# Queries copied by GpSimd one unit sooner in an attention backward loop, their transposing DMA ahead of the second score transpose of a block

## The chip, the cores and the metric

One core of one Trainium2 chip. The metric is the device time of the slowest (here the only) core, in microseconds. The engines: PE does matmuls (PEld loads their weights), DVE, ACT and POOL (GpSimd) work elementwise, SP issues DMAs. Each engine takes its instructions in order, and waits on semaphores for the others.

## What is computed

Two attention blocks on a sequence of 2048 tokens of 448 features with 16 heads of 28, and the gradients of all their inputs. Block A is linear attention, block B softmax attention with one key head and one value head for all query heads. The change lies in block B's loop:

```python
q = (x @ wq).reshape(B, S, H, Dh)        # 16 heads
k = x @ wk                               # one head of keys
v = x @ wv                               # one head of values
scores = einsum("bhqd,bkd->bhqk", q, k) * Dh ** -0.5
p = softmax(scores)
o = einsum("bhqk,bkd->bhqd", p, v)
b = o.reshape(B, S, H * Dh) @ wo
# the output is concatenate([a, b]); vjp(grad_out) gives the gradients of x, wq, wk, wv, wo of both blocks
```

With E the exponentials of the scores and dS = E * (v . do - D), the loop makes o (E with v), dv (E with do), dq (dS with k) and dk (dS with q) for each pair of heads.

## The kernel before, in words

The first fifth of the time is block A and what block B's loop needs; it is not touched. Then a loop written out by hand, with its order fixed (`manual_schedule`, line 922), runs over *units* u = 0 to 539 (line 931). A unit is 256 keys (two tiles of 128) of one *block*; a block is 256 queries of one pair of heads and has 8 units, so there are 64 blocks and 512 units of scores. Later stages of the same unit of work come later in the loop: the gradient of unit w = u - 16, the transpose of unit y = u - 18, and so on. In a unit:

- PE makes the scores of u and the products v . do of w (`rows_SD`, line 683), and by parity of u the sums for o and dq (`o_dq`, line 894) or those of dk (`dk_m`, line 865).
- ACT takes the exponentials of the two score banks into eT (lines 955 and 997), and copies one bank of v . do into cp (line 971).
- DVE multiplies the other bank by eT into half 0 of dsT (line 967); POOL multiplies cp by eT into half 1 (line 972). dsT has 5 buffers, cp has 3.
- DVE transposes dsT of unit u - 18 in 32 x 32 blocks into dsx (line 1041), that is, two units after POOL's product of the same piece. dsx feeds dk on PE.
- After units 3 and 7 of a block SP issues a transposing DMA, eN from eT of four units (line 999; 1 MiB). eN feeds dv on PE: `dv_mm` (line 901) for block b begins at unit 8b + 20. There are 5 buffers of eT and 6 of eN.
- Once a block, on POOL: prod (line 821), don and o (lines 830 and 831) in unit 2 of the following stage, Dq and its product (lines 836 and 837) in unit 4. In every fourth block or so POOL also issues an output DMA (line 749).
- After blocks 15, 31, 47, 55 and 63 SP issues a transposing DMA of the outputs o (line 1048).

dk needs the queries in another layout, qX, made anew for each chunk of 256 queries (eight blocks, 64 units); there are two buffers of it. For each of four groups g of heads, POOL copies the queries in two halves into a staging tile qst (`qc_copy`, lines 854 to 857; called at line 979), and one transposing DMA on SP's queue brings qst into qX (`qc_T`, lines 859 to 861; called at line 1002). There is **one buffer** of qst (line 709), so the first copy of a group waits until the DMA of the group before has read it. The first chunk is made ahead of the loop (lines 924 to 930); the other seven in blocks 3 to 6 of each eight, four groups each, 28 in all, up to unit 447 (`u < 448`). The first dk that reads a new qX comes 27 units after its chunk's first unit.

The places of copies and DMA follow from one line: in unit u, `gq` is the group and `iq` the unit counted from the group's first; copies run at iq 0 and 1, behind the product of the same unit on POOL, and the DMA is issued at iq 1, behind the eN transpose if the unit has one.

```python
gq, iq = divmod(u % 64 - 30, 8)
...
    if iq < 2:
        qc_copy(nc.gpsimd, qst, qq, gq, iq)
...
    if u % 4 == 3:
        nc.sync.dma_start_transpose(ENs[u // 4 % 6][:, :, :],
...
    if 0 <= gq < 4 and iq == 1 and u < 448:
        qc_T(qst, qq, gq)
```

Before, the copies stand in units 6 and 7 of a block, and the DMA in unit 7 behind that unit's eN transpose.

Of the kernel before, what the change touches and what calls it, by code (L numbers as in the profile page):

```python
# [25 lines left out]
def kernel(  # L26
# [624 lines left out]
    with ExitStack() as cs_:  # L651
# [270 lines left out]
        with tc.manual_schedule():  # L922
# [8 lines left out]
            for u in range(NU + 28):  # L931
# [31 lines left out]
                if hasD:  # L963
# [6 lines left out]
                    cp = pc_.tile([P, 512], BF16, name="cp")  # L970
                    nc.scalar.activation(out=cp[:, :], in_=dp[1][:, :], func=ACT.Copy)  # L971
                    nc.gpsimd.tensor_tensor(out=dst[:, 1, :], in0=cp[:, :], in1=ew[:, 1, :], op=ALU.mult)  # L972
                gq, iq = divmod(u % 64 - 30, 8)
                qq = u // 64 + 1
                if 0 <= gq < 4 and u < 448:
                    if gq == 0 and iq == 0:
# [183 lines left out]
```

## Time and profile before

| | |
|---|---|
| median of 3 runs | 1047.6 us (1046.28 to 1047.8) |
| the profiled execution | 1045.81 us, its span 1044.1 us |
| granted TensorE clock | 1.0 |
| busy: PE, DVE, ACT, POOL | 1003.6, 887.4, 865.8, 811.9 us |
| POOL's products, line 972 | 512 at 1156 ns mean |
| POOL's copies into qst, line 856 | 56 at 613 ns mean |
| eN transposes issued by SP, line 999 | 128, median 5422 ns each |
| qst transposes issued by SP, line 860 | 28, median 1264 ns each |
| DMA traffic | 195.15 MB, mean 187 GB/s |

How to read it: the profile lists busy time by engine and by line of the kernel, and for each group of instructions the idle time of its engine ahead of them, with what ended it. A row of SP's queue (SPq) is the time that SP takes to issue the transfer; when it has landed is told by the completion events of its semaphore. An arrow out<-in names the tile written and those read. "[2.11 <-X]" behind a row of the timeline is idle time of that engine before it, and X ended it as far as the profile can tell.

### The profile page before, as it was taken

The page shows a single profiled execution, that of the slowest core. Times are in us where ns is not written, and L with a number is a line of the kernel's source. Part 1 is how long each engine was busy: PE and PEld are TensorE (multiplying, and loading weights), DVE is VectorE, ACT ScalarE, POOL GpSimd, SP SyncE. Part 2 cuts the span into 40 slices and gives each one's busy share as a digit, 9 for nine tenths or more (in the row PEclk, how much of TensorE's full clock was granted, in tenths as well). Part 3 has the DMA queues.
Part 4 walks back from the last instruction along what each step waited for, and adds up shares of the span by engine and source line. Part 5 has one row for each costly group of instructions (what it writes and reads, how often), then busy time and mean ns, then how long its engine had stood idle before and what let it go on. Part 6 is the DMA issues. An engine that isn't in the chain of part 4 may idle for free.

```text
span 1044.1 us, 40103 instructions
## 1 busy us (share of the span) xinstructions
PE 1003.6 (96%) x16236; PEld 485.1 (46%) x16245; DVE 887.4 (85%) x1780; ACT 865.8 (83%) x1743; POOL 811.9 (78%) x1106
## 2 busy tenths in 40 slices
PE   9999999998899999999999999999999999999998
PEld 5555555434444444444444444444444444444444
DVE  7898500669899999999999999999999999999942
ACT  6463132599999999999999999999999999999632
POOL 8601282238898999999999989999998999888860
PEclk9999999999999999999999999999999999999999
DMA  9879999199999999999999999999999999999983
GB/s 266 150 134 195 184 232 213 32 161 205 189 183 198 191 188 195 198 190 189 201 198 197 190 190 203 194 193 198 202 184 201 191 199 192 192 194 197 218 159 90
DMA packets 689059, 195.15 MB, mean 187 GB/s; under 512 B 670409, under 2 KB 686689, under 8 KB 688873
## 3 DMA queue, kind: packets, MB, share of 16 engines
q1 hardware_dynamic: 680392, 179.97, 103.7%
q0 software_dynamic: 4544, 9.46, 3.1%
q10 hardware_dynamic: 3936, 3.16, 1.1%
q8 instruction: 127, 2.08, 0.8%
q14 instruction: 60, 0.48, 0.2%
HBM read 12.60 MB, written 10.84 MB: 22 GB/s over the span
## 4 chain that ended last, share of the span: by engine, by line
PE 37%; DVE 28%; POOL 17%; issue 9%; ACT 8%; DMA 0%; DVEq 0%; POOLq 0%; ACTq 0%
PE agen L81 13%; POOL dsT L972 12%; DVE dsT L967 12%; DVE dsx L1041 10%; PE agen L676 8%; PE aacc L676 7%; PE aacc L81 6%; ACT cp L971 4%; ACT eT L997 2%; DVE doT L852 1%; DVE R L986 1%; POOL qst L856 1%; POOL prod L821 1%; PE aacc L809 1%; DVE Dq L835 1%
## 5 line engine op out<-in xcount | busy, mean ns | idle before, releaser
L972 POOL TENSOR_TENSOR dsT<-cp,eT 128x512 bf16<-128x512 bf16 x512 | 584.1, 1156 | 45.5 <-ACT cp L971 39.8
L1041 DVE STREAM_TRANSPOSE dsx<-dsT 128x512 f32<-128x512 f32 x512 | 357.2, 698 | 8.7 <-POOL dsT L972 5.9
L676 PEld LDWEIGHTS <-R 32*128 32x128 bf16 (+1 forms) x9104 | 245.1, 94 | 246.5 <-issue 195.4
L967 DVE TENSOR_TENSOR dsT<-agen,eT 128x512 bf16<-128x512 f32 x512 | 340.3, 665 | 9.7 <-PE agen L676 4.1
L971 ACT ACTIVATE cp<-agen 128x512 bf16<-128x512 f32 x512 | 326.2, 637 | 12.2 <-PE agen L676 10.3
L955 ACT ACTIVATE eT<-aacc 128x512 bf16<-128x512 f32 x512 | 325.3, 635 | 12.6 <-PE agen L676 6.7
L997 ACT ACTIVATE eT<-aacc 128x512 bf16<-128x512 f32 x512 | 332.4, 649 | 0.0
L676 PE MATMUL agen<-dsx,qX 32*32 32x512 bf16 x4024 | 264.0, 376 | 0.0
L676 PE MATMUL agen<-doT,R 32*128 32x256 bf16 x2048 | 241.6, 269 | 4.1 <-DVE dsT L967 2.6
L676 PE MATMUL aacc<-R,R 32*128 32x256 bf16 (+1 forms) x2240 | 208.3, 267 | 18.9 <-DVE doT L852 7.5
L676 PE MATMUL agen<-dsT,R 128*32 128x256 bf16 x2048 | 155.8, 273 | 0.3 <-POOL dsT L972 0.2
L676 PE MATMUL agen<-eT,R 128*32 128x256 bf16 x2048 | 155.7, 273 | 0.1
L676 PEld LDWEIGHTS <-qX 32*32 32x32 bf16 x4096 | 78.2, 89 | 112.4 <-issue 54.1
L676 PE MATMUL aacc<-eN,don 128*32 128x512 bf16 x1024 | 90.6, 387 | 0.0
L81 PEld LDWEIGHTS <-R 128*128 128x128 bf16 x517 | 40.9, 98 | 41.4 <-issue 11.0
L856 POOL COPY qst<-R 128x512 bf16<-128x512 bf16 x56 | 34.3, 613 | 11.2 <-DMA qX<-qst 5.7
L81 PE MATMUL agen<-R,R 128*128 128x448 bf16 (+1 forms) x174 | 41.1, 360 | 1.7 <-issue 0.6
L676 PEld LDWEIGHTS <-don 128*32 128x32 bf16 x1024 | 20.9, 93 | 40.6 <-issue 40.6
L821 POOL TENSOR_TENSOR prod<-R,oTs 128x128 f32<-128x128 bf16 x64 | 27.5, 430 | 9.0 <-DVE oTs L817 9.0
L586 DVE TENSOR_TENSOR osb<-R 32x512 bf16<-32x512 bf16 x4 | 1.7, 414 | 35.4 <-ACT R L583 35.4
L262 POOL TENSOR_SCALAR wdq<-wdq 128x448 bf16<-128x448 bf16 x16 | 21.1, 1327 | 12.8 <-DVE phiT L243 12.8
L427 POOL COPY pk<-R 128x256 bf16<-128x256 bf16 x4 | 1.6, 400 | 37.7 <-DVE R L389 37.7
(235 smaller groups left out, 1001.2 us busy)
## 6 DMA issues: line engine op xcount, KB each, us to landing
eN<-eT SPq DMA_TRANSPOSE x128
xa<-in_A_x_dram SPq DMA_DIRECT2D x8, 224.0 KB
ga<-in_grad_out_dram SPq DMA_DIRECT2D x4, 448.0 KB
out_dram<-osb ACTq DMA_DIRECT2D x16, 112.0 KB
xa<-in_grad_out_dram POOLq DMA_DIRECT2D x4, 448.0 KB, 8.3
out_dram<-wdq POOLq DMA_DIRECT2D x8, 224.0 KB, 5.1
eT<-in_grad_out_dram SPq DMA_DIRECT2D x4, 448.0 KB
eT<-in_B_x_dram SPq DMA_DIRECT2D x4, 448.0 KB
```

Source lines behind the costliest of these rows:

```text
L81: nc.tensor.matmul(out_ap, lhsT=lhsT, rhs=rhs, start=start, stop=stop, tile_position=(0, 0))
L262: nc.gpsimd.tensor_scalar(out=wq_n[:, st, 0:D], in0=wq_n[:, st, 0:D], scalar1=1.0, scalar2=None, op0=ALU.min)
L676: nc.tensor.matmul(out, lhsT=lhsT, rhs=rhs, start=start, stop=stop, tile_position=pos, skip_group_check=True)
L809: nc.tensor.transpose(onp[:, qb, :, :].rearrange("p h c -> p (h c)"), oTs[0:64, qb * P:(qb + 1) * P], identF[0:64, 0:64], tile_position=(0 ...
L821: nc.gpsimd.tensor_tensor(out=prod[b][:], in0=dnv, in1=os_, op=ALU.mult)
L856: eng.tensor_copy(out=st.rearrange("p (b s) a j -> p b s a j", s=2)[:, :, s, :, :], in_=src.unsqueeze(2).to_broadcast([P, 4, 4, 32]))
L955: nc.scalar.activation(out=eT(u)[:, 0, :], in_=sp[0][:, :], func=ACT.Exp, scale=scale)
L967: nc.vector.tensor_tensor(out=dst[:, 0, :], in0=dp[0][:, :], in1=ew[:, 0, :], op=ALU.mult)
L971: nc.scalar.activation(out=cp[:, :], in_=dp[1][:, :], func=ACT.Copy)
L972: nc.gpsimd.tensor_tensor(out=dst[:, 1, :], in0=cp[:, :], in1=ew[:, 1, :], op=ALU.mult)
L997: nc.scalar.activation(out=eT(u)[:, 1, :], in_=sp[1][:, :], func=ACT.Exp, scale=scale)
L1041: nc.vector.transpose(out=dsx[b][:, tp, :, :, :].rearrange("p h t c -> p (h t c)").bitcast(F32), in_=dsT[y][:, :, :].rearrange("p h c -> p ...
```

## The change

The group's first unit moves from 30 to 29 (of 64):

```diff
-                gq, iq = divmod(u % 64 - 30, 8)
+                gq, iq = divmod(u % 64 - 29, 8)
```

With it move, in all 28 groups: the two copies on POOL from units 6 and 7 of a block to units 5 and 6, and the DMA of qst from unit 7, where it stood behind the eN transpose, to unit 6, where no eN transpose is issued; so in SP's order it now stands between the eN transposes of units 3 and 7. The choice of the qX buffer moves along by one unit. Nothing else changes: the order of instructions on PE, DVE and ACT is the same, and as many instructions run.

## Prediction

> **What bounds the kernel now.** I read the page first (busy shares, DMA queues, costliest groups), then POOL's waits, then SP's and POOL's timelines around the copies, then DVE's.
>
> ```profile
> PE 1003.6 (96%) x16236; PEld 485.1 (46%) x16245; DVE 887.4 (85%) x1780; ACT 865.8 (83%) x1743; POOL 811.9 (78%) x1106
> ...
> q1 hardware_dynamic: 680392, 179.97, 103.7%
> ...
> L856 POOL COPY qst<-R 128x512 bf16<-128x512 bf16 x56 | 34.3, 613 | 11.2 <-DMA qX<-qst 5.7
> ```
>
> PE is busy nearly throughout, and one DMA queue, SP's, fills the DMA engines. The copies cost 34.3 us on POOL, and POOL stood idle 11.2 us ahead of them. POOL's waits between 250 and 900 us split that:
>
> ```profile
> POOL qst L856 <- DMA qX<-qst: 5.7, 7, 1.6
> POOL qst L856 <- DVE dsx L1041: 3.4, 2, 2.1
> POOL qst L856 <- DVE dsT L967: 2.1, 1, 2.1
> ```
>
> All ten waits are for the same thing. The trace's completion events of the DMA from qst come at 266.28 and 280.10 us, the copies put down to DVE start at 266.34 and 280.15: there is one qst, and the next copy waits until the transpose has read it. POOL's timeline at the first (start, duration, idle before):
>
> ```profile
> 260.85 3.38 POOL L972 TENSOR_TENSOR dsT<-cp,eT 128x512 bf16<-128x512 bf16 x3
> 266.34 0.61 POOL L856 COPY qst<-R 128x512 bf16<-128x512 bf16 x1 [2.11 <-DVE dsx L1041]
> 266.90 1.15 POOL L972 TENSOR_TENSOR dsT<-cp,eT 128x512 bf16<-128x512 bf16 x1
> 268.00 0.61 POOL L856 COPY qst<-R 128x512 bf16<-128x512 bf16 x1
> ```
>
> The products (line 972) behind the copy are late, and two units later DVE's transposes (line 1041) wait for them:
>
> ```profile
> 268.09 0.71 DVE L1041 STREAM_TRANSPOSE dsx<-dsT 128x512 f32<-128x512 f32 x1 [0.85 <-POOL dsT L972]
> ```
>
> What it costs: from ACT's line 955, eight units (a block) take 11.77 to 11.84 us where nothing disturbs them, 1.47 a unit. Blocks 5, 6, 15, 22, 23, 36 to 39, 53 and 55, each with such a wait in it or just before, are longer by 1.4, 1.9, 0.9, 0.4, 0.8, 0.3, 0.7, 0.2, 1.4, 1.2 and 0.2 us: **9.2 us** in all.
>
> Why the DMA is late, SP's timeline says:
>
> ```profile
> 261.92 1.27 SPq L860 DMA_TRANSPOSE qX<-qst  x1
> 263.35 11.56 SPq L999 DMA_TRANSPOSE eN<-eT  x2
> 274.97 1.31 SPq L860 DMA_TRANSPOSE qX<-qst  x1
> 276.39 10.64 SPq L999 DMA_TRANSPOSE eN<-eT  x2
> 287.14 1.96 SPq L860 DMA_TRANSPOSE qX<-qst  x1
> 289.55 10.76 SPq L999 DMA_TRANSPOSE eN<-eT  x2
> ```
>
> SP issues without a pause. Every DMA of qst goes behind the eN transposes of units 3 and 7 of its block, and starts 3.4 to 7.5 us after its second copy has ended. From 214 to 732 us no gap between SP's transposes exceeds 0.55 us. So in this stretch SP's calendar is fixed by its own work: a block with a qst DMA needs 2 x 5.42 + 1.26 + three gaps of some 0.08 = 12.3 us, more than the block's 11.8; one without needs 11.0, and the lag is worked off.
>
> **The change part by part.** It removes and adds no instruction: 56 copies and 28 DMAs each move. On POOL the two copies go ahead of the products of units 6 and 7 instead of 7 and the next 0 (the orders on PE, DVE and ACT stay). On SP the DMA of qst moves past one eN transpose.
>
> *Gain.* The DMA is issued one eN sooner, 5.4 us, and the next copy asks one unit sooner, 1.47 us: 5.4 - 1.47 = 3.9 us more slack at the copy. The longest wait is 2.1 us, so at unchanged pace all ten go, and with them 9.2 us.
>
> *What is late next: the same queue.* Its calendar does not move when compute gets faster. So what compute saves, S, comes off its distance to the DMAs that it reads. I worked out two kinds of cap from the trace.
> (a) The matmuls on eN (the rows aacc<-eN,don, first of each block) against the landing of their later eN: margins are mostly 5 to 9 us, the smallest after 250 us being 4.2 at 428 us (block 16), **3.5 at 618 us** (block 32), 5.3 at 809, 5.2 at 906. The low ones follow the o transposes (line 1048, 2.9 to 3.1 us), which lie in the same queue. In copy blocks the eN of unit 7 now goes 1.26 + 0.1 = 1.4 us later; the smallest margin there, 5.9, becomes 4.5.
> (b) The copies. A product may start about 1.4 us behind its cp before DVE feels it (start lag plus DVE's spare is 1.6 to 1.9 us in the undisturbed block 28, and the second copy adds 0.57 - 0.36 = 0.2). Against that allowance the old landings are late by 1.2 and 1.9 us (266, 280 us), 0.7 (387), 0.4 and 0.6 (470, 483), 0.2 and 1.2 (661, 674) and 0.4 (840). Each plus 3.9 is the room now: 2.7, 2.1, 3.2, 3.5, 3.3, 3.7, 2.8, 3.5.
>
> Summing in order: blocks 5 and 6 give back 1.4 + 1.9 = 3.3 (at 280 us S is 1.4, the room 2.1). At 387 S 3.3 meets room 3.2: of 0.9 0.8 comes, S = 4.1. At 470 and 483 the rooms 3.5 and 3.3 take about as much as the 0.4 and 0.8 to be had: S stays 4.1. At 618 cap (a) cuts it to 3.5. Blocks 36 to 38 give 0.3 + 0.7 + 0.2 to S = 4.7; the room 2.8 at 674 makes a loss of 1.9 where 1.4 was: S = 4.2. At 732 SP has some 0.6 us of pauses that a later stream uses up, so rooms grow by that; block 53 gives 1.2, a remainder near 864 us takes 0.5: **S = 4.8**. The caps 5.2 + 0.5 at 906 hold. I take 4.6, a little off for blocks with an output DMA on POOL (0.55 to 0.58 us), below.
>
> *The copies' place on POOL, and the cost if cover goes.* POOL recovers 1.47 - 1.11 = 0.36 us a unit. Before, lags of the products in an undisturbed copy block run 0.94, 1.02, 0.66, 0.28 in units 3 to 6 (behind prod, don, R and Dq), then 0.47 and 0.68 behind the copies. Now the copies come where 0.66 is left: 0.87, then 1.08, then 0.72. DVE's spare covers it: nothing lost. Behind an output DMA the lag is 0.4 higher: 1.3, then 1.55, against 1.6: cost 0, a tenth missing.
>
> *SP's wait at its new place.* It waits for the second copy, and all eN behind it would stand. SP comes there 5.4 us sooner, the copy ends 1.47 sooner: of the old lags 3.4 to 7.5 us, 3.9 is used. With S above 1 none waits; with S = 0 the two shortest (734, 746 us) would pause SP 0.6 and 0.4 us, hidden under eN margins of 6 to 8 us. Cost 0; ends 0 and 1. The eN issue itself is bounded by its row:
>
> ```profile
> L999 SPq DMA_TRANSPOSE eN<-eT x128: 4810/5422/6142, 214.4 to 972.4; - x128
> ```
>
> Even after 942 us, where SP waits for each eT, single transposes take 4.8 to 5.4 us; so pace is no matter of crowding, and the calendar stands. The tile is 128 x 4096 bf16, 1.05 MB: 193 GB/s, as the page's GB/s row. The Trainium skill, page "DMA: Bandwidth & Descriptors", section "Latency and other measured facts", gives a DMA transpose an effective 261 GB/s, which would be an estimated 4.0 us here; by that the queue would have room and the change would keep the whole gain. The measured 5.42 us decides against it.
>
> **The sum.** The profiled execution: 1045.81 us (span 1044.1 and 1.7 around it) - 4.6 = 1041.2. It lies 1.8 below the median of the runs, 1047.6, which I forecast from: 1047.6 - 4.6 = **1043.0**.
>
> **Rivals.**
> 1. *The queue leaves the gain alone* (compute runs ahead, and eN and qX come sooner than the fixed calendar says): all 9.2 us, 1038.4. For it: ten waits ahead of copies are the only long idle time in the loop. Against: SP without a pause for 500 us and 5.42 us apiece. This is also where the Trainium skill's 261 GB/s would lead. 0.13.
> 2. *The queue takes nearly all*: the time comes back as PE's waits for eN at blocks 16 and 32, or as waits for qst at 387 to 483 and 674 us, since caps of 2.8 to 3.5 us hang on single landings that vary by a microsecond (qst DMAs land 3.3 to 5.1 us after issue). S ends between 0 and 2: some 1046.5. 0.17.
> 3. *Slower: POOL's peak lag passes DVE's spare.* The copies now follow the four small operations by one unit instead of two; the peak goes from 0.68 to 1.08 us, to 1.55 behind an output DMA. It decides at 1.6 us. Should copy blocks run 0.5 us above my lags, each of 28 blocks loses about 0.3 us, 8.4 us, against 4.6 gained: 1051.4. For it: a tenth of a microsecond is left in some blocks. Against: one block in four has that DMA, and all others have 0.5 to spare. 0.10.
>
> That the change does nothing is excluded by the order on POOL, which it moves in all 28 groups.
>
> **How the numbers follow.** Forecast 0.60, rivals 0.13, 0.17 and 0.10. The range 1038.2 to 1048.2 takes in rivals 1 and 2 and the drift between execution and median; rival 3 and the tails are left out. About 0.2%, 2.1 us, is what a measurement of this kernel tells from no change. Faster: forecast and rival 1 nearly whole, 0.73 and a little of rival 2: 0.76. Same: 0.14. Slower: 0.10.
>
> **What would show it.** Right: the idle time ahead of line 856 falls from 11.2 us to under 5; SP's timeline reads eN, qX, eN without pauses; blocks 5 and 6 take 11.8 us; and PE's waits show eN landings near 618 us, where none were. Wrong: an SP that pauses (then the calendar was not fixed), eN durations under 5 us, DVE's waits for line 972 above the present 5.9 us, or POOL's copies waiting as before.

## The result, and the profile after

Before 1047.03 us, after **1043.53 us** (medians of 6 runs each): 3.5 us less, a ratio of 0.9967, interval 0.9955 to 0.9979. In a second comparison the changed kernel ran at 1042.61 us, ratio 0.9954 (0.9939 to 0.9969). The profiled execution took 1044.09 us, span 1042.4.

The page of the changed kernel, the lines that answer to those of before:

```profile
PE 1003.5 (96%) x16245; PEld 485.1 (47%) x16245; DVE 886.9 (85%) x1780; ACT 865.2 (83%) x1743; POOL 812.3 (78%) x1106
...
q1 hardware_dynamic: 680392, 179.97, 105.0%
...
L856 POOL COPY qst<-R 128x512 bf16<-128x512 bf16 x56 | 34.2, 611 | 5.0 <-DVE dsx L1041 2.5
```

No engine does more or less; idle time ahead of the copies is 5.0 us where it was 11.2. The waits between 250 and 900 us (us in all, times, longest), POOL's for qst and then PE's:

```profile
POOL qst L856 <- DVE dsx L1041: 2.5, 2, 1.3
POOL qst L856 <- DMA qX<-qst: 2.5, 4, 1.1
```

```profile
PE aacc L676 <- DVE doT L852: 4.9, 25, 0.5
PE aacc L676 <- DVE oTs L817: 3.0, 6, 0.6
PE agen L676 <- DVE dsT L967: 1.1, 3, 0.6
PE aacc L676 <- DMA eN<-eT: 1.0, 2, 0.8
```

The kernel before has no line like the last one: PE now waits for landings of eN. SP's timeline shows the new order, a qst DMA between the two eN transposes of a block (a pair "x2" is now unit 7's and the next block's unit 3), and as little pause as before; the largest gap between transposes from 214 to 942 us is 0.46 us:

```profile
245.58 10.37 SPq L999 DMA_TRANSPOSE eN<-eT  x2
256.05 1.26 SPq L860 DMA_TRANSPOSE qX<-qst  x1
257.41 11.04 SPq L999 DMA_TRANSPOSE eN<-eT  x2
268.51 1.30 SPq L860 DMA_TRANSPOSE qX<-qst  x1
269.92 10.74 SPq L999 DMA_TRANSPOSE eN<-eT  x2
280.78 1.24 SPq L860 DMA_TRANSPOSE qX<-qst  x1
```

POOL at the copy that waited 2.11 us at 266 us before: it comes at 262.54, behind two products, with no idle time, 2.8 us after the landing.

```profile
260.34 2.27 POOL L972 TENSOR_TENSOR dsT<-cp,eT 128x512 bf16<-128x512 bf16 x2
262.54 0.62 POOL L856 COPY qst<-R 128x512 bf16<-128x512 bf16 x1
263.11 1.16 POOL L972 TENSOR_TENSOR dsT<-cp,eT 128x512 bf16<-128x512 bf16 x1
264.21 0.61 POOL L856 COPY qst<-R 128x512 bf16<-128x512 bf16 x1
```

Where the time went, by lengths of blocks from ACT's line 955 (us before, us after, and what compute has gained since block 2 by the end of these blocks):

| block | before | after | gained by its end |
|---|---|---|---|
| 5 | 13.2 | 11.8 | 1.4 |
| 6 | 13.7 | 11.8 | 3.2 |
| 15 | 12.7 | 12.1 | 3.9 |
| 22, 23 | 12.2, 12.6 | 12.5, 12.8 | 3.3 |
| 36 to 39 | 12.0, 12.5, 12.0, 13.2 | 11.8, 12.9, 12.6, 11.9 | 3.9 |
| 43 | 11.8 | 12.5 | 3.1 |
| 50 | 11.8 | 12.8 | 2.1 |
| 53, 54 | 13.0, 11.8 | 11.8, 13.0 | 2.0 |

The early waits are gone for good; from block 22 on waits stand again, in blocks 43, 50 and 54 where there were none. At block 50 it is eN (PE's timeline: the six matmuls that begin with the first read of block 48's later eN start on its landing at 807.0 us; in the trace before, the same eN landed at 804.2), in block 54 again qst:

```profile
805.85 0.39 PE L676 MATMUL aacc<-eN,don 128*32 128x512 bf16 x2
807.04 0.61 PE L676 MATMUL aacc<-eN,don 128*32 128x512 bf16 x6 [0.80 <-DMA eN<-eT]
```

```profile
844.94 2.27 POOL L972 TENSOR_TENSOR dsT<-cp,eT 128x512 bf16<-128x512 bf16 x2
848.37 0.61 POOL L856 COPY qst<-R 128x512 bf16<-128x512 bf16 x1 [1.16 <-DVE dsx L1041]
```

(That landing is at 848.31; DVE is named, but the DMA ended the wait.) At 720 us, block 43, PE stood 0.8 us ahead of weight loads without a wait that the profile shows; it is not in the second profile of this kernel, and its cause stays open. In that second profile no wait of PE for eN shows at all: the copies alone wait, 6.5 us, and the gain at the loop's end is 1.9 us, against 1.8 here.

### The profile page after: what moved, and what is told of

The parts are those of the page before. It is cut to its first block, busy times and chain, and to the rows that moved or that the text cites. A ratio compares the mean times of both kernels' runs of the same rounds, so it can differ in the third digit from the quotient of the medians.

```text
span 1042.4 us, 40109 instructions
## 1 busy us (share of the span) xinstructions
PE 1003.5 (96%) x16245; PEld 485.1 (47%) x16245; DVE 886.9 (85%) x1780; ACT 865.2 (83%) x1743; POOL 812.3 (78%) x1106
## 4 chain that ended last, share of the span: by engine, by line
PE 39%; DVE 25%; POOL 16%; ACT 8%; issue 7%; DMA 3%; DVEq 0%; SPq 0%; ACTq 0%; POOLq 0%
PE agen L81 13%; POOL dsT L972 12%; DVE dsT L967 10%; PE agen L676 9%; DVE dsx L1041 9%; PE aacc L676 8%; PE aacc L81 7%; ACT cp L971 4%; ACT eT L997 2%; DMA eN<-eT 2%; DVE doT L852 1%; DVE R L986 1%; POOL qst L856 1%; POOL prod L821 1%; PE aacc L809 1%
## 5 line engine op out<-in xcount | busy, mean ns | idle before, releaser
L971 ACT ACTIVATE cp<-agen 128x512 bf16<-128x512 f32 x512 | 327.0, 639 | 11.8 <-PE agen L676 9.7
```

## Experiments

The theory: SP's queue is full, so its *calendar* (the times at which its DMAs start and land) is fixed, and compute gains until it runs into landings of eN (at dv) or of qst (at the copies). Rivals: the copies' place on POOL matters; or leads do not matter, and the queue's total work alone sets the end.

**The two parts apart.** e1_dma_only, from the kernel before: the two statements change places, so the DMA goes ahead of unit 7's eN, and the copies stay.

```diff
+                    if 0 <= gq < 4 and iq == 1 and u < 448:
+                        qc_T(qst, qq, gq)
                     if u % 4 == 3:
                         nc.sync.dma_start_transpose(ENs[u // 4 % 6][:, :, :],
...
-                    if 0 <= gq < 4 and iq == 1 and u < 448:
-                        qc_T(qst, qq, gq)
```

> One part alone: the copies stay in units 6 and 7 as before; only the DMA of qst goes ahead of unit 7's eN transpose instead of behind it. Theory (SP's calendar of transposes is fixed; compute gains until it runs into landings of eN or of qst): the copies ask 1.47 us later than in the changed kernel while the DMA lands no later, so the room at the copies is 1.5 us more and only the margins at eN cap the gain, near 618, 720 and 809 us: 1042.0, between 1040.5 and 1043.5, idle time ahead of line 856 under 2 us. Rival (the place of the copies on POOL is what gains): no better than before, 1047. Rival (SP stands at the DMA until the second copy of unit 7 is done, all eN behind it): pauses of SP of about 1 us in each of 28 groups, 1047 or more.

Measured: 1043.06 us against 1047.91, ratio 0.9949 (0.9931 to 0.9967). Waits in it that bear on this, 250 to 910 us:

```profile
PE aacc L676 <- DMA eN<-eT: 3.0, 4, 1.3
POOL qst L856 <- DMA qX<-qst: 1.2, 2, 0.7
...
DVE dsx L1041 <- POOL dsT L972: 0.2, 1, 0.2
```

As expected: the copies hardly wait, and PE's four waits for eN (at 615, 782, 806 and 866 us) are the cap. SP made no pauses. The DMA's place alone brings as much as the whole change: against the changed kernel the difference is within the intervals.

e2_copies_only, from the changed kernel: the DMA back to unit 7, behind eN.

```diff
-                    if 0 <= gq < 4 and iq == 1 and u < 448:
+                    if 0 <= gq < 4 and iq == 2 and u < 448:
```

> The other part alone: the copies go to units 5 and 6 as in the changed kernel, the DMA of qst stays in unit 7 behind the eN transpose. Theory (fixed calendar): the landings stay where they were and each copy asks 1.47 us sooner, so compute is held back about 1.5 us further in all, once and not per group: 1048.5, between 1047.5 and 1050, with more than 20 us idle ahead of line 856. Rival (each of 21 groups loses its 1.47 us anew): 1060 or more. Rival (the copies' new place on POOL gains): 1045 or less.

Measured: 1051.01 us against 1047.91, ratio 1.0029 (1.0017 to 1.0041): 3.1 us slower where 1.5 was expected, and above the stated range, which ended at 1050.

```profile
POOL qst L856 <- DMA qX<-qst: 12.0, 13, 2.8
DVE dsx L1041 <- POOL dsT L972: 7.7, 11, 2.0
...
POOL qst L856 <- DVE dsx L1041: 1.0, 1, 1.0
```

Idle time ahead of the copies is 13 us, not over 20. The direction holds, the size does not, and 21 groups do not each lose 1.47 us. The unit that the copies move gains nothing; with the DMA at its old place it costs.

**Room in the queue.** e3_half_before and e4_half_after, in the kernels before and after:

```diff
-                        nc.sync.dma_start_transpose(ENs[u // 4 % 6][:, :, :],
-                                                    ETs[u // 4 % 5][:, :, :, :].rearrange("p a b c -> p (a b c)"))
+                        nt = 4 if u < 24 else 2
+                        nc.sync.dma_start_transpose(ENs[u // 4 % 6][:, 0:8 * nt, :],
+                                                    ETs[u // 4 % 5][:, 0:nt, :, :].rearrange("p a b c -> p (a b c)"))
```

> Kernel before, but from unit 24 on each eN transpose moves half of its tile only (512 KiB; the other half keeps old values, so dv is left incomplete). The queue then needs about 2 x 2.7 + 1.3 us in a block of 11.8. Theory (the full queue delays the DMA of qst): all ten waits ahead of the copies and all 9.2 us of longer blocks go: 1037.8, between 1036.5 and 1039. Rival (what cost the time before is POOL's load in the blocks with copies, not the queue): 1045 or more.

> Changed kernel with the same halved eN transposes from unit 24 on (dv incomplete). Theory (the full queue is what took back two thirds of the gain): 1037.8, the same as the kernel before with halved transposes within 1 us: with room in the queue the change is worth nothing, and nothing is lost by the copies' place on POOL. Rival (the copies now too close behind POOL's small operations are what took gain back): 1041 or more, above the other one. Rival (the place of the copies gains by itself): 3.5 us below the other one.

Both leave half of each eN, and so part of dv, undone. Measured: 1036.98 us, ratio 0.9897 (0.9882 to 0.9912), and 1037.37 us, ratio 0.9901 (0.9885 to 0.9916). In neither does a copy wait; both gain 8.8 us in the loop. With room in the queue the change is worth nothing, and the copies' new place costs nothing either. (A halved transpose also waits for two units of eT instead of four, and so may go out 2 x 1.47 = 2.9 us sooner; what this does by itself was not separated from the smaller load.) The windows view, 265 to 725 us (length, busy time of PE, PEld, DVE, ACT and POOL, clock, DMA share, GB/s; the share adds up the times of packets and can pass 1), for the kernel after and then for e3:

```profile
265.00:725.00 460.00, 445.76 (x8822) 210.63 (x8818) 448.97 (x887) 456.50 (x928) 429.47 (x547) 1.00 1.20 193
```

```profile
265.00:725.00 460.00, 448.94 (x8922) 213.34 (x8910) 451.98 (x894) 459.72 (x936) 433.30 (x551) 1.00 0.65 107
```

and SP's timeline of e3, which now pauses (from 266 us on):

```profile
266.49 1.24 SPq L860 DMA_TRANSPOSE qX<-qst  x1
267.82 7.70 SPq L1000 DMA_TRANSPOSE eN<-eT  x2
278.30 1.24 SPq L860 DMA_TRANSPOSE qX<-qst  x1
279.99 7.50 SPq L1000 DMA_TRANSPOSE eN<-eT  x2
```

Halving the tiles brings the DMA share from 1.20 to 0.65, and with it comes the time that the change could not fetch.

**Spreading the load.** e7_spread, from the changed kernel; e9_spread_old is the same with 30 and 478 in place of 29 and 477.

```diff
-                gq, iq = divmod(u % 64 - 29, 8)
-                qq = u // 64 + 1
-                if 0 <= gq < 4 and u < 448:
+                gq, iq = divmod((u - 29) % 64, 16)
+                qq = (u - 29) // 64 + 1
+                if 29 <= u < 477:
...
-                    if 0 <= gq < 4 and iq == 1 and u < 448:
+                    if iq == 1 and 29 <= u < 477:
```

> Changed kernel, but the four groups of a chunk are 16 units apart instead of 8 (copies in units 5 and 6 of every second block, the last group in block 1 of the next eight; all the work is done). SP's work is the same in all, but no longer four blocks in a row of 12.3 us against 11.8. Theory (the gain was cut by the queue's lag, which peaks behind four copy blocks and the o transposes): no wait for qst at all, lags of eN stay under 8 us instead of 9 to 10.8, and most of the 9.2 us comes: 1038.5, between 1037 and 1041. Rival (SP's total work from 214 to 942 us sets the end, wherever it lies): as the changed kernel, 1043.5.

> Kernel before (copies in units 6 and 7, DMA behind unit 7's eN transpose) with the groups 16 units apart. Theory: with 23 us between groups no copy waits for qst, whatever the order of SP's DMAs, and the unit that the change moves is worth nothing: within 1.5 us of the other spread kernel, 1038.5, between 1037 and 1041. Rival (the place of DMA and copies matters in itself): 3.5 us above the other spread kernel.

Measured: 1045.73 us against 1048.59, ratio 0.9970 (0.9955 to 0.9985), and 1043.75, ratio 0.9957 (0.9944 to 0.9971). The expectation failed: no copy waits in either, and still only about 3 to 5 us come. PE's waits for eN, first in e7, then in e9:

```profile
PE aacc L676 <- DMA eN<-eT: 2.5, 4, 1.2
```

```profile
PE aacc L676 <- DMA eN<-eT: 4.1, 5, 1.6
```

By block 40 they have gained 5.6 and 5.8 us (e9 after a wait for eN of 1.5 us at 615), and by the loop's end 2.6 and 3.2: PE's waits for eN at 699 us (e7), 805 to 829 and 903 us stand between. Spreading moves no work out of the queue: in the long run compute can be no further ahead than dv's lead over the landings allows. The rival of these two expectations, that the queue's total work sets the end, gave the changed kernel's time, and by the times alone it is not excluded.

**Sooner still, and the changed kernel again.** e8_sooner puts 28 in place of 29.

> Changed kernel with the group one unit sooner still: copies in units 4 and 5, right behind the small operations of POOL, DMA in unit 5, still between the eN transposes of units 3 and 7. Theory: SP's calendar gives the same landings, each copy asks 1.47 us sooner, so the room at the copies is 1.5 us less (as before the change plus 2.4), and POOL's peak lag rises to 1.44 us, to 1.9 behind an output DMA, over the 1.6 that DVE spares: 1045.5, between 1044 and 1047.5, with 8 to 15 us idle ahead of line 856. Rival (sooner is better, the DMA's slot free of eN is all that counts): 1043.5 or less.

> The changed kernel once more, unchanged, on the chip of this comparison. By its first runs: 1043.5, between 1042 and 1045; the runs scatter by more than a microsecond, by the theory because its end hangs on single landings of the full queue, while kernels with room in the queue scatter by half a microsecond.

Measured: e8 1042.89 us, ratio 0.9956 (0.9939 to 0.9973), and the changed kernel again 1042.61 us. The loss of 2 us that the theory gave e8 is not seen; its copies stood idle 2.8 us, not 8 to 15. The higher lag on POOL cost nothing either: e8's first copy blocks, 4 to 6, take 11.81 to 11.84 us, as in the changed kernel. For the landings the calendars suggest a reason. From the start of the 9th eN transpose to that of the 113th, with no gap of SP over 0.55 us, single executions took:

| kernel | calendar, us | gained at the loop's end | gained + (calendar - 623.3) |
|---|---|---|---|
| before | 623.3 | 0 | 0 |
| after | 625.7 | 1.8 | 4.2 |
| after, again | 625.8 | 1.9 | 4.4 |
| e1 DMA only | 624.7 | 3.1 | 4.5 |
| e7, e9 spread | 625.7, 625.4 | 2.6, 3.2 | 5.0, 5.3 |
| e8 sooner | 622.5 | 3.6 | 2.8 |
| e2 copies only | 626.8 | -4.2 | -0.7 |

The work is the same but for e7 and e9, where one qst transpose less falls into this stretch (some 1.4 us; with it their last column is 6.4 and 6.7). SP's DMAs come in one order in the kernel before, e2 and e14 (below; 629.1 us, also without a pause), and in one order in the changed kernel, e1 and e8. So calendars differ by up to 1% with the same order: 623.3 to 629.1 and 622.5 to 625.8 us. What sets them stays open. Only the changed kernel was profiled twice, and its two agree within 0.1 us, so a cause in the timing of each kernel's compute is not excluded. With room in the queue (e3, e4) compute passes the same stretch in 617 us, so even at the fastest calendar the queue is the slower of the two.

That a late landing comes off the gain can be followed at block 48. Its later eN had 5.3 us to spare before; less the 3.1 gained by then, less 0.5 by which this trace's loop began sooner, less the 2.8 that it landed later (807.0 against 804.2), -1.1 is left, and PE waits. The last column takes it for the whole loop, microsecond for microsecond, which is argued and not shown. By it e8 lies 1.5 us below the changed kernel, as one unit less of room would have it, and e2, at -0.7, is nearer its -1.5 than its time is. It is worked out of single executions and is no measurement of its own; by the times e8 and the changed kernel cannot be told apart.

**The lead of dv.** e11 to e14 begin dv two units later, in the changed kernel, in e9, in e1 and in the kernel before.

```diff
-                    b, n = divmod(u - 20, 8)
+                    b, n = divmod(u - 22, 8)
```

> Changed kernel, with the matmuls that read eN (dv) begun two units later, at unit 8b + 22 instead of 8b + 20; all the work is done. That gives compute 2.9 us more lead over the landings of eN and none over those of qst. Theory (two caps on the lead over a fixed calendar): the waits for eN at 720 and 807 us go, waits for qst stay or grow: 1042, between 1040 and 1043.5. Rival (total work of the queue alone sets the end, leads do not matter): 1043, as the changed kernel.

> Copies in units 6 and 7 as before the change, groups 16 units apart (no wait for qst possible), and dv two units later. Only the cap at eN is left, and it is 2.9 us higher. Theory: 3 us better than the spread kernel without it: 1040, between 1038 and 1042, no or few waits of PE for eN. Rival (total work of the queue alone): 1043 to 1044, as without.

> The DMA-only kernel (copies in units 6 and 7, DMA of qst ahead of unit 7's eN transpose) with dv two units later. Both caps are wide: at the copies 5.4 us less the old lateness, at eN 2.9 more. Theory: better than the DMA-only kernel by 2 to 3 us: 1040.5, between 1038.5 and 1042.5. Rival (total work of the queue alone): as without, 1043.

> Kernel before with dv two units later. There no PE wait for eN stood in the trace, only waits for qst. Theory: a higher cap at eN is worth nothing where the copies are the cap: 1047.5, between 1046 and 1049, the same idle time ahead of line 856, 9 to 13 us. Rival (later dv helps by itself, by the order on PE): 2 us or more better.

Measured: e11 1047.88 us against 1047.67, ratio 1.0004 (0.9994 to 1.0014); e12 1047.86, 1.0002 (0.9993 to 1.0011); e13 1048.18, 1.0006 (0.9998 to 1.0015); e14 1050.69, 1.0033 (1.0020 to 1.0047). All four miss. A cost appeared that I had not allowed for: undisturbed blocks take 11.93 to 11.98 us instead of 11.77 to 11.84, some 0.17 us in each, 10 us in the loop, with PE waiting more for DVE's products (e11, 250 to 900 us):

```profile
PE agen L676 <- DVE dsT L967: 6.8, 28, 0.3
```

(0.4 us in 2 waits in the kernel before). So they do not settle what a longer lead is worth, and the rival of the total work stays open with it. They do show the other side of the queue: at 12.0 us a block compute no longer outruns it, no PE waits for eN, and three kernels with different orders of copies and DMA agree within 0.3 us. Only with the old order (e14) do copies still wait, 12.1 us as expected, and it is 2.8 us slower than e11.

## Why the prediction came out

**Direction and mechanism: right.** The ten waits were for the one qst, the DMA was late for its place behind unit 7's eN (e1), and a full queue took back 5.7 of the 9.2 us, or 4.4 by the second comparison. e3 and e4 show the last: with room in the queue both kernels come to 1037, 1.0 to 1.4 us below the 1038.4 that I gave for an unhindered gain. Gained by block 6: 3.3 forecast, 3.2 measured; by block 15 4.1 and 3.9. The 9.2 itself was a little high: the eleven figures listed for it add up to 9.4, and the loops of e3 and e4 gain 8.8. Block 15 takes 12.1 us there too and block 39 11.9, so 0.4 us of their length was no wait for qst.

**Size: -4.6 forecast, -3.5 measured (interval -2.2 to -4.7), -4.8 by the ratio of the second comparison.** By these times the 4.6 is not shown to be off. By the traces the sum is: its 4.8 at the loop's end stands against 1.8 and 1.9 measured, so that the medians came near the forecast is in part luck: the execution profiled before, from whose trace I took the sum, was 1.2 us faster than its kernel's median of six, the one after 0.6 slower. The step that was mis-sized is "SP's calendar is fixed". No pause of SP moved it, but the stretch took 2.4 us longer after (625.7 against 623.3), and eN landings between 740 and 930 us came later than in the one execution that I took the margins from, by a median of 2.2 us (for unit 7's eN in copy blocks, 1.4 of that is the change's own). With the longer calendar added back the measured gain is 4.2 to 4.4, near the sum's 4.8. The scatter fits a queue whose pace varies, though no run shows that it comes from there: the changed kernel's six runs lie between 1041.7 and 1044.28 us, 31 of the kernel before in the last comparison between 1044.2 and 1052.14, the four of each halved one within 0.7.

**Caps: right in kind, off in place.** Cap (a) was to bite at 618 us; the margin there was 0.5 us, with that landing 0.9 us earlier than in the trace of before, and it bit at 807, where I had let the 5.3 hold, as it would have by the old landing. Cap (b) bit at 464 to 478, 643 to 656 and 848 us, near the forecast's 470, 674 and 864. (The o transposes that I gave 2.9 to 3.1 us took 1.8 and 1.2 us ahead of 809 and 906.)

**The copies' unit.** I counted 1.47 us against the change, rightly: e1, without that part, waits 1.2 us at the copies instead of 5.0, and e2, with it alone, is slower. That POOL's peak lag stays covered was right: e4 equals e3. SP's wait at the new place cost nothing, as said: no gap over 0.46 us.

**The rivals.** The unhindered gain (rival 1) is excluded by the times; e3 and e4 reach it only with room in the queue. Rival 2, the queue taking nearly all, is not what the medians show, but the two traces end where it said, at an S between 0 and 2, and by its reason, single landings that vary; the places were others, 807 and 848 us. Rival 3 (slower by POOL's lag) did not occur.

This case's queue moves 193 GB/s; the 261 GB/s that the Trainium skill, page "DMA: Bandwidth & Descriptors", section "Latency and other measured facts", gives a DMA transpose whose middle dimension is not contiguous were not reached by whole tiles. For the halved ones SP's median issue is 2.05 us (e3) and 2.34 us (e4) for 512 KiB, 256 and 224 GB/s by issue time, so the remark that pace is no matter of crowding went too far: where SP waited after 942 us the transpose before was still landing (in the trace before, the one issued at 936.4 us landed at 944.1, after the next was issued at 942.3).

**The signs.** Blocks 5 and 6 take 11.8 us, SP's timeline reads eN, qX, eN without pauses, and DVE's waits for line 972 fell from 5.9 to 3.2 us, as said. The idle time ahead of line 856 stopped at 5.0 us, and at 6.5 in the second profile, where I had said under 5; and no wait for eN showed near 618 us.

## What to carry to other kernels

Where one in-order DMA queue issues without a pause, removing a wait for it buys only the lead up to the next landing that something reads: work out that margin at every reader before you count the gain. Putting a short transfer ahead of a long one frees its reader and adds no work to the queue, but spreading or reordering does not shorten the queue either. Of the edits tried here only less work in it did, at the price of an incomplete dv; against the kernel before that was worth 8.8 us in the loop and 10.5 to 10.9 us by the medians. Take the margins from several executions, since calendars here differ by as much as the gain in question.

## What the runs showed of the hardware that was not expected

Halving a transpose of 1 MiB cut SP's median issue from 5.42 to 2.05 us in e3 and 2.34 in e4, more than half; landing came 4.2 to 4.3 us after the issue began in a quarter of e3's (median 4.8), instead of 6.7 to 10. And with its DMAs in the same order the full queue took 623.3 to 629.1 us in one order and 622.5 to 625.8 in the other for 104 eN transposes and what lies between, up to 1% apart, while the runs of each kernel with halved transposes lie within 0.7 us.
